# Strassen moved between products of two interleaved layers: input product of the last FFN in all four chunks, K instead of Q in layer 2

## The chip, the cores and the metric

The kernel runs on one core of a Trainium2 chip. The metric is the device time of one execution in microseconds (us), as the median of several executions; lower is better. Profiles are of one execution each. Some executions of a program come out slower, with a lower granted clock in the records. Every ratio is of fast executions alone.

In the text PE is TensorE, PEld its weight loads, DVE is VectorE, ACT is ScalarE, POOL is GpSimd and SP is SyncE, which issues the DMA transfers.

## The reference, cut to what matters

```python
def reference(A_x, A_wqkv, A_wo, B_x, B_w1, B_w2):      # x: 1 x 2048 x 512, bf16; w1: 512 x 1376
    def _A_ref(x, wqkv, wo):                             # linear attention, 32 heads of 16
        q, k, v = ...                                    # x @ wqkv
        phi = lambda t: jnp.where(t > 0, t + 1, jnp.exp(t)) + 1e-6
        pq, pk = phi(q), phi(k)
        kv = jnp.einsum("bhsd,bhse->bhde", pk, v)
        z = jnp.einsum("bhsd->bhd", pk)
        num = jnp.einsum("bhqd,bhde->bhqe", pq, kv)
        den = jnp.einsum("bhqd,bhd->bhq", pq, z)[..., None] + 1e-6
        return ...(num / den) @ wo
    def _B_ref(x, w1, w2):
        return jnp.maximum(x @ w1, 0) @ w2
    x = A_x
    x = x + _A_ref(_layernorm(x), A_wqkv, A_wo)          # layer 0
    x = x + _B_ref(_layernorm(x), B_w1, B_w2)            # layer 1
    x = x + _A_ref(_layernorm(x), A_wqkv, A_wo)          # layer 2
    x = x + _B_ref(_layernorm(x), B_w1, B_w2)            # layer 3, "the last FFN"
    return x
```

## The kernel before

The 2048 rows are four chunks of 512. The kernel first records all operations with what they read and write. A table in the source (`ORDER`) then gives the order in which they are dealt out to the engines, another (`BANKS`) the PSUM bank of each accumulator, and the waits follow from the data and the banks. Each engine runs its own list strictly in that order.

Some products are done by one level of Strassen: 7 block products of half the size in place of 8. The block sums of x and of the weights and some of the outputs cost DVE and ACT work. This is one group of the FFN's Strassen product (layer 3 did chunks 1 to 3 so, chunk 0 plain):

```python
f32s = [(lden[:, 0, :], ...), (lden[:, 1, :], ...), (rhi ... F32, ...), (rsp[:]....bitcast(F32), [("rsp", 0), ("rsp", 1)])]

def f32_slot(layer):                     # scratch for the copy c6, taken in turn
    L = f32s[1:] if layer == 1 else f32s
    ...
tt(0, blk(0, 0), blk(0, 1), ALU.add, TK[0])              # tb0: block sums of the transposed x, on DVE
tt(1, TS[0], blk(1, 1), ALU.subtract, TK[1] + tk[0])     # tb1
...
X, Z = alloc_bank(full), alloc_bank(full)
prod("p1", w_raw(0, 1), t_sum(0), X, True)               # PE
prod("p6", w_sum(4), t_raw(1, 1), Z, True)               # PE
s6, k6 = f32_slot(layer)
copy(lambda: s6[:, 0:W], Z, [], k6, "c6")                # PSUM -> scratch, ACT or DVE
Y = alloc_bank(full, seeded=True)
copy(bank_ap(Y), X, [], [("ps", Y)], "c11")              # PSUM -> PSUM
prod("p2", ..., X);  prod("p5", ..., Y);  relu(Y, 0, 0)
V = alloc_bank(full, seeded=True)
g.add(DVE, ... psv[:, V] = psv[:, X] + s6 ...)           # c21
prod("p4", ..., X);  prod("p3", ..., V);  relu(V, 1, 0)
U = alloc_bank(full, seeded=True)
copy(bank_ap(U), X, ..., "c12")
g.add(DVE, ... out_ap(1, 1) = pv(X) + s6 ...)            # hadd: frees bank X
g.add(DVE, ... max(out_ap(1, 1), 0) ...)                 # hq
prod("p7", ..., U);  relu(U, 0, 1)
```

An operation's name carries its chunk and the first feature tile of its group: hadd0_0 is the hadd of chunk 0, first group. Q and K of attention have the same scheme.

Of the kernel before, what the change touches and what calls it, by code (L numbers as in the profile page):

```python
# [9 lines left out]
F32 = mybir.dt.float32  # L10
# [122 lines left out]
17 0 14 12 15 18 13 1 16 19 2 20 22 3 24 4 21 23 25 5 6 26 27 7 28 8 29 40 30 33 31 32a 41 34 47 42 35 71 43 36 48 44  # L133
49 37 45 50 73 38 46d 72 51 81 74 39a 75 52 54 82 76 53a 60 83 86 58 78 56 87 77 79 61 57 55 98 59 89 62 84 63 119 88
93 99 115 100 108 64 66d 95 65d 67a 103 80 69 117 68a 92 85 90 94 113 70 135 105 91 104 116 120 141 114 118 121 110
180 122 109 251 174 130 176 123 136 132 127d 124d 131 125d 142 138 126d 128 178 137 148 143 179 133 181 129 175 144
169 177 134 182 149 96 183 106 159 111 171 112 170 97 147 107 160 101 161 184 191 185d 186a 187d 139 164 140 150 189
172 192 153 173 165 151 239 188d 193 154 102 190 166 145 162 203 155 163 167 156 9 152 209 194 10 205 157 195 11 204
197 146 210 158 196 206 199 207 198 240 221 200 168 211 201 215 223 212 213 222 233 224 217 225 216 227 218 234 219
235 202 428 228 208 229 236 237 252 230 231 253 427 254 214 255 322 282 323 242 220 283 243 226 324 241 284 232 325  # L140
245 285 238 244 246 326 250 247 259a 329 248 249 257d 256a 260 286 258a 287 270 262 327 289 261 280 263 328 330 272
264 288 271 265 281 290 314 267 273 320 291 275 315a 333 331 321a 318 268 316 277 319d 294 317a 332 266 309 293 274
296 292 395 311 269 278 310 297 400 396 295 276 397 410 401 398a 279 405 402 411 403a 339 412 406 413a 415 334 407 340
408a 383 335 343 349 416 341 336 338 337d 344 350 342a 299 351 353 345 354 384 429d 304 346 352d 301 347d 433 300 424
355 434 436a 465 430d 306 466 449 425 435a 450 305 426 437 468a 438 385 356 298 421 312 451a 431d 386 470 348 432d 469
369 471d 439a 302 422d 399 371 307 423 303 404 377 372d 467a 414 389 440 363 388 378a 308 442 390 364a 313 441 472 387
443a 357 481 370d 444a 473 474 417 409 358 375 359 445 475a 476a 447 446 418 482 393 373 477 376a 392 365 483 394 448d
374a 484 367 452a 391 478 366a 419 498 368d 420 493 499 486 502 503 494 487 500 497 508 485 501d 495 488 504 496a 381
509 507 513 379 510 512 490 505 506d 479 511a 454 491 453 489 382a 514 515 360 380a 492 456 480a 519 361a 545d 455a
524 362 520 529 525 523 546d 566 528 534 567a 530 549 533 547d 458 550a 548d 603 459a 457 604a 598d 568 460a 599d 551  # L150
569 602 552 570 461 553 571 605a 463 554 572 462 464a 601d 555 535 573a 618 556a 674d 538 607 578 526 608a 675d 561
527a 600d 606 521 621d 522a 562 609 579 539 563 677d 557 574 564 580 558 581 565 678 559 575 679a 622 582 576 680 560
623 681 634 536 624a 583 682 637d 577 537d 610 683 638 613a 611 584 531 585 532d 639 612a 684 586 676d 540 587 640a
616 685a 614 695 617a 619 588 751d 696a 595 591d 620a 615 592a 697 625 690 596a 698 594 589a 627 516 590d 626 628a
752d 635 593 699 754d 636a 753d 629a 686 700 691 630 597 701 641 632 702a 631 642 517 541 633a 643 518 542 687 644d
692 707 645a 693 703 646 694 648 647 708 649a 688 755 803d 689 662 758a 804d 756 664 772 757a 805d 704 759 773a 709
806d 663 760 807 761a 705 650 808a 762 706 771 710 652 763 651 774d 809 711 712 764 766d 775 765a 810 769 665 713 811
770a 714 715 666 716 776 812 656 777a 778 717 813 719a 720d 780 814d 658 779 543 767 544 718a 819 653 781d 824 782a
722 787 654 657 815 783 825a 785 659 668 790d 786a 721d 792 768 670 723 791 793d 826 669 784 660 816 748 827 817 828
749a 671 818 788 829 724 750 789d 794 830 726 672 796 725 831d 795 820 797d 798a 727 832 728 836 799 837 800 801 730  # L160
802a 873d 736 732 731 874d 821 833 738 838 655 737 875d 877 876d 661 822 667 834 878a 823 839 879 835 894 880 840 673
895d 841 842 843 881 733 844 734 845 896 882 729 897 739 846 898 849d 850a 848d 883 847d 852 735 899 884d 900 740 851
1066 889 1065 890 1068 1067 885 901d 891 902 892 886 903 893 887 742 904 888 906 744 907 743 908 745 868 905 909 746
910 741 911 912 1069 869 747 913 914 870 915 858 871 872 943 916 860 920d 853 859 919d 861 922 958 855 862 918d 854
863 917d 959 856 921 960 944 857 865 948 961 864 962 953 866 950 867 949 933 951 954 952 955 968 935 956 934 928 957
936 937 969 930 929 923 931 932 938 924 925 945 939 970 926 940 927 963 941 942 980 965 964 946 966 982 971 967 981
947 983 972 984 985 973 995 974 987 975 1000 986 988 997 1001 989 996 1070 998 990 999 1071 978 1002 992 976 991 979
1005 993 1004 1072 1025a 977 1006 994 1003 1024a 1027 1023d 1026a 1073 1011 1029 1009 1047 1028 1030 1007 1012 1074
1048 1075 1077a 1010 1049 1013 1076d 1051 1078 1050a 1008 1053 1014 1055 1031 1054a 1032 1052d 1056d 1037 1034 1084
1033 1133 1039 1035 1015 1036 1038 1123 1017 1134 1018 1135 1118 1124 1016 1136a 1040 1128 1127 1125 1119 1126a 1019  # L170
1085 1120 1129 1042 1121a 1130 1022 1091a 1086 1138 1021 1044 1079 1020 1131d 1097 1043 1045 1182 1087 1139 1041 1046
1081 1167 1183 1080 1088 1184 1057 1168 1098 1172 1099 1169 1170d 1177 1058 1173 1137 1174 1147 1175d 1059 1100 1187
1082 1122 1149 1089 1090 1148a 1178 1159 1132 1060 1150d 1185a 1155 1179 1101 1180a 1083 1161 1092 1156a 1188 1196d
1151 1093 1162d 1094 1216 1189 1140 1152a 1063 1141 1200 1095 1171 1062 1096 1157 1142 1061 1203d 1160a 1143 1064
1219d 1106 1158a 1153 1107 1197d 1176 1163 1199d 1104 1154a 1165 1103 1108 1164d 1181 1201 1109 1102 1166a 1144 1105
1198d 1202a 1204 1300d 1186 1205 1207 1220 1145a 1232 1206a 1111 1193 1302d 1113 1235a 1217 1301d 1194a 1110 1208
1218a 1112 1209 1303d 1195 1236 1210a 1221 1223 1319 1222a 1146 1190 1248 1191 1117 1211a 1192 1115 1225 1114 1212
1224 1226a 1214 1116 1320a 1253 1213 1215a 1249 1321 1227a 1250 1251d 1237 1252 1258 1322 1254 1238a 1230 1255 1257
1323 1256d 1259 1231a 1263 1268 1324 1262 1304 1260 1264 1325 1265 1267 1261d 1233 1279 1305d 1326a 1266d 1234a 1228
1306 1269 1327 1307 1239 1330 1338d 1308 1280 1331 1309 1283 1241 1229 1240 1242d 1310 1243a 1281 1282a 1339d 1274  # L180
1311d 1244 1342 1275 1246 1343 1247a 1340d 1315 1345a 1245 1341d 1344a 1284 1390d 1278 1312 1285 1316 1391d 1288 1347
1276 1346 1392d 1277a 1358 1328 1349 1348a 1317 1294 1313 1332 1393d 1361a 1350 1351 1286 1333 1363 1352a 1362 1270
1364a 1271 1287d 1394 1353a 1272 1318 1273 1359 1329 1356 1360a 1289 1428d 1395a 1365 1357a 1396 1290 1366 1354 1335
1369a 1293 1397 1367 1291 1374 1336a 1292d 1398 1355 1368a 1295 1296 1372 1399 1375 1370 1377a 1400 1373a 1337 1379
1376d 1401a 1409 1371 1380a 1297 1405 1298 1314 1410a 1299 1402 1432 1411 1334 1429d 1435a 1431d 1378 1433 1412 1406
1430d 1434a 1413 1381 1437 1414 1382 1438a 1383 1415 1384a 1385d 1436 1416a 1386 1465 1403 1466a 1407 1387 1449 1404
1448 1450a 1439 1388 1420 1389a 1408 1451a 1421 1480d 1441 1440 1442a 1482d 1452 1443a 1464 1481d 1453 1467a 1417
1454a 1444 1446 1484 1447a 1445 1455 1422 1469 1485a 1468 1483d 1470a 1457 1418 1458a 1423 1499 1486 1471 1500a 1419
1456 1473 1487 1501 1424 1459a 1472 1474a 1502 1488 1460 1425 1461 1475a 1503 1489 1426a 1476 1462 1427 1490 1477
1463a 1504 1478 1517d 1491a 1505 1479a 1495 1506a 1515d 1496 1510 1516d 1497 1511 1498 1519 1518d 1534 1520a 1507  # L190
1535a 1521 1536 1522 1508 1537 1512 1523 1509 1538 1524 1492 1539 1513 1525 1540 1526a 1493 1541a 1530 1494 1527 1514
1528 1542 1529 1543 1545 1554 1544 1546 1531 1547 1555 1532 1548 1549 1533 1550 1551 1553 1552
# [1265 lines left out]
```

## Time and profile before

| | before |
|---|---|
| time, median (range) | 271.12 us (270.93 to 271.31, 3 runs) |
| span of the profiled execution | 269.3 us |
| granted PE clock | 1.0 |
| DVE / ACT busy | 86% / 73% |

PE is busy 98% of the span. Because shown matmul times overlap, this document counts PE otherwise: from the start of one group's first weight load to the start of the next group's, less the turns of its matmuls (216 ns for 512 columns, 109 for 256; the prediction derives both from the timeline). What is left over is **waiting**. PE's own work in before is 259.3 us by this count and its waits come to 5.5 us, of which 3.1 us lie before 11 us, while inputs arrive. Weight loads serve for it because none of their records is missing. The count has an artefact: about 0.3 us at each group of small denominator products (their turn is uncertain), in all kernels alike, except where such a group lies at the border of two stages: it can then be counted on either side, and this is said. Only differences between kernels are used.

A line of a timeline gives start us, length us, engine, line, operation, output and inputs, count; in brackets the idle time before it and its releaser.

```profile
199.09 0.42 DVE L964 TENSOR_TENSOR xn<-xn,Tb 128x512 f16<-128x512 f16 x1 [1.06 <-DMA Tb<-xn]
...
197.79 2.76 PE L539 MATMUL ps<-Tb,w 128*128 128x512 bf16 x12
```

DVE stood 1.06 us, from 198.0 to 199.1, for a transposing transfer. PE did not notice: it was in the middle of twelve plain products of FFN chunk 0, which need nothing but transposed x and weights.

### The profile page before, as it was taken

How to read it: one execution, taken by the hardware profiler on the slowest of the kernel's cores; microseconds unless marked ns; L12 is line 12 of the kernel's file. 1: busy time of each engine (PE TensorE's matmuls, PEld its weight loads, DVE VectorE, ACT ScalarE, POOL GpSimd, SP SyncE). 2: the span in 40 equal slices, each digit the busy share in tenths (PEclk: the TensorE clock that was granted, in tenths of full speed). 3: DMA queues.
4: the chain of work that ended last, by engine and by line, in shares of the span. 5: the costliest groups of instructions: out<-in, count | busy, mean ns of one | idle time of the engine just before them, and what ended most of it. 6: DMA issues, size and time to landing. Idle time of an engine off the chain costs nothing.

```text
span 269.3 us, 5317 instructions
## 1 busy us (share of the span) xinstructions
PE 263.8 (98%) x1973; PEld 170.5 (63%) x1973; DVE 232.6 (86%) x635; ACT 196.1 (73%) x426; POOL 18.8 (7%) x30
## 2 busy tenths in 40 slices
PE   7999999999999999999999999999999999999995
PEld 2444454447556879778666544455458677888884
DVE  4999975999989999999799765599989999979865
ACT  3889956999978768787542887899998757656420
POOL 4111000000110002111010100000011001100000
PEclk9999999999999999999999999999999999999999
DMA  6954973254343027204004060215356222320204
GB/s 209 382 112 79 241 259 102 93 80 99 97 134 63 2 40 87 52 1 80 19 2 78 0 82 1 74 57 126 78 139 118 41 39 41 58 82 0 100 0 156
DMA packets 47481, 23.60 MB, mean 88 GB/s; under 512 B 36736, under 2 KB 46048, under 8 KB 47456
## 3 DMA queue, kind: packets, MB, share of 16 engines
q1 hardware_dynamic: 47312, 23.21, 35.1%
q8 instruction: 15, 0.25, 0.4%
q14 instruction: 10, 0.08, 0.1%
q10 hardware_dynamic: 144, 0.07, 0.1%
HBM read 11.21 MB, written 3.15 MB: 53 GB/s over the span
## 4 chain that ended last, share of the span: by engine, by line
PE 92%; DVE 3%; DMA 3%; ACT 1%; issue 0%
PE ps L539 92%; DMA Tb<-xn 2%; DVE bst L446 1%; DMA xin<-in_A_x_dram 1%; DVE xn L478 0%; DVE xn L579 0%; ACT sqscr L546 0%; DVE xn L1166 0%; PE ps L502 0%; DVE mv L447 0%; ACT escr L521 0%; ACT big L519 0%; DVE Tb L510 0%; DVE big L525 0%; DVE xn L1126 0%
## 5 line engine op out<-in xcount | busy, mean ns | idle before, releaser
L521 ACT ACTIVATE escr<-ps 128x512 bf16<-128x512 f32 x60 | 35.7, 606 | 7.8 <-PE ps L539 7.8
L546 ACT ACTIVATE sqscr<-xres 128x512 bf16<-128x512 f32 x48 | 30.4, 634 | 14.5 <-DVE xres L583 7.6
L519 ACT ACTIVATE big<-ps 128x512 bf16<-128x512 f32 x60 | 35.1, 606 | 1.0 <-PE ps L539 1.0
L539 PE MATMUL ps<-wqkv,Tb 128*128 128x512 bf16 x128 | 31.2, 379 | 1.0 <-DMA Tb<-xn 0.5
L1015 ACT ACTIVATE big<-ps 128x512 bf16<-128x512 f32 (+1 forms) x47 | 24.9, 536 | 9.6 <-PE ps L539 8.8
L539 PE MATMUL ps<-big,xn 128*128 128x512 bf16 x128 | 30.9, 379 | 0.0
L539 PE MATMUL ps<-gw,big 128*128 128x512 bf16 x128 | 30.3, 379 | 0.0
L539 PE MATMUL ps<-Tb,wqkv 128*128 128x512 bf16 x112 | 27.0, 379 | 0.0
L525 DVE TENSOR_TENSOR big<-big,escr 128x512 bf16<-128x512 bf16 x60 | 24.6, 421 | 2.4 <-ACT big L519 1.5
L523 DVE TENSOR_SCALAR escr<-escr 128x512 bf16<-128x512 bf16 x60 | 16.9, 287 | 9.2 <-ACT escr L521 8.8
L539 PE MATMUL ps<-w2s,big 128*128 128x256 f16 x160 | 21.9, 273 | 0.0
L539 PEld LDWEIGHTS ps<-wqkv,Tb 128*128 128x128 bf16 x128 | 12.0, 98 | 14.6 <-DMA Tb<-xn 1.0
L539 PEld LDWEIGHTS ps<-big,xn 128*128 128x128 bf16 x128 | 12.2, 98 | 13.8 <-issue 0.4
L539 PE MATMUL ps<-w,big 128*128 128x256 f16 (+2 forms) x113 | 20.6, 302 | 0.0
L539 PEld LDWEIGHTS ps<-gw,big 128*128 128x128 bf16 x128 | 12.2, 98 | 12.8 <-issue 0.5
L539 PE MATMUL ps<-w,xin 128*128 128x256 bf16 (+1 forms) x140 | 19.5, 273 | 0.0
L539 PE MATMUL ps<-xn,xin 128*128 128x256 f16 x128 | 19.5, 272 | 0.0
L998 ACT ACTIVATE ps<-ps 128x512 f32<-128x512 f32 (+1 forms) x28 | 14.6, 521 | 5.7 <-PE ps L539 2.8
L539 PEld LDWEIGHTS ps<-Tb,wqkv 128*128 128x128 bf16 x112 | 10.8, 98 | 12.5 <-issue 0.2
L539 PE MATMUL ps<-xn,w 128*128 128x256 f16 x120 | 18.7, 273 | 0.0
L539 PE MATMUL ps<-Tb,w 128*128 128x512 bf16 x80 | 18.4, 379 | 0.0
L539 PE MATMUL ps<-Tb,wper 128*128 128x256 bf16 x120 | 18.3, 273 | 0.0
(152 smaller groups left out, 512.0 us busy)
## 6 DMA issues: line engine op xcount, KB each, us to landing
xn<-rdram SPq DMA_DIRECT2D x32, 128.0 KB
wqkv<-in_A_wqkv_dram SPq DMA_DIRECT2D x3, 512.0 KB, 7.2
xin<-in_A_x_dram SPq DMA_DIRECT2D x3, 512.0 KB, 8.0
out_dram<-xn SPq DMA_DIRECT2D x3, 512.0 KB, 2.6
w<-in_B_w_dram SPq DMA_DIRECT2D x1, 1376.0 KB, 6.7
w<-in_B_w_dram SPq DMA_DIRECT2D x1, 1280.0 KB, 9.8
rdram<-rsp SPq DMA_DIRECT2D x8, 128.0 KB, 1.7
wo<-in_A_wo_dram SPq DMA_DIRECT2D x1, 512.0 KB, 10.2
```

What stands on the lines that cost most here:

```text
L446: g.add(DVE, lambda e: e.bn_stats(bst[:, i, :], xin[:, i, :]), [("xin", i)] + list(behind), [("bst", i)], C_DVE_BNST, name="bnst%d" % i)
L519: g.add(ACT, lambda e: e.activation(dst_ap, psv[:, b, :], ACTF.Identity, bias=1.0 + 1e-6, scale=1.0), [("ps", b)], [dst_key], C_ACT_PSUM, ...
L521: g.add(ACT, lambda e: e.activation(escr[:, s, :], psv[:, b, :], ACTF.Exp), [("ps", b)], [("escr", s)], C_ACT_EXP, name=name + "_exp")
L523: g.add(DVE, lambda e: e.tensor_scalar(escr[:, s, :], escr[:, s, :], 1.0, 1e-6, ALU.min, ALU.add), [("escr", s)], [("escr", s)], C_DVE_BF4 ...
L525: g.add(DVE, lambda e: e.tensor_tensor(dst_ap, dst_ap, escr[:, s, :], ALU.max), [dst_key, ("escr", s)], [dst_key], 340.0, name=name + "_phi")
L539: last = e.matmul(o, l, r, start=st, stop=sp, skip_group_check=skip)
L546: g.add(ACT, lambda e: e.activation(sqscr[:, q, :], xres[:, i, :], ACTF.Square, accum_out=dst[:, i:i + 1]), [("xres", i)], [("sqscr", q), ...
L998: g.add_flex([(ACT, lambda e: e.activation(dst(), psv[:, src, 0:W], ACTF.Identity), cost(C_ACT_PSUM)), (DVE, lambda e: e.tensor_copy(dst() ...
L1015: g.add_flex([(ACT, lambda e: e.activation(out_ap(r, m), pv(b), ACTF.Relu), cost(C_ACT_PSUM)), (DVE, lambda e: e.tensor_scalar(out_ap(r, m ...
```

## The change

The intent is fewer PE turns: Strassen also for chunk 0 of the last FFN's input product, K of layer 2 by Strassen in chunks 2 and 3, Q of chunk 3 of layer 2 plain again. The order, the banks and some scratch places go with it. The core of the diff, with cuts marked:

```diff
 ORDER = """                       # all 1600 operations in a new order; BANKS likewise
...
-QSTR=(3,), ... KSTR=(), ... HSTR=[(1, 2, 3), (1, 2, 3)]
+QSTR=(), ... KSTR=[(), (2, 3)], ... HSTR=[(1, 2, 3), (0, 1, 2, 3)]
...
-   ... 750.0 * (hi - lo), "tr%d" % lo, issue=C_SP_TR)      # guess of a transpose's transfer, for the order only
+   ... 950.0 * (hi - lo), "tr%d" % lo, issue=C_SP_TR)
...                                                         # sums and scratch of K get places of their own:
+   home = [xn[:, 4 * t + k, :] if kind == "q" else unit_ap(pq_unit(k, t)) for k in range(4)]
...
+   else:
+       s6 = big[:].bitcast(F32).rearrange("p (c t k) -> p c t k", t=NCH, k=256)[:, 8:10, 2, :]
...
-                        if layer == 2 and t in KSTR:
+                        if t in KSTR[layer // 2]:
```

## The prediction

> **What bounds the kernel now.** I began with the busy shares of the page.
>
> ```profile
> PE 263.8 (98%) x1973; PEld 170.5 (63%) x1973; DVE 232.6 (86%) x635; ACT 196.1 (73%) x426; POOL 18.8 (7%) x30
> ...
> PEclk9999999999999999999999999999999999999999
> ```
>
> The TensorE (PE) is busy nearly always, at full clock in every slice. A busy PE can still be starved, because the shown time of a matmul is longer than its turn in the pipeline. So next I read the chain that ended last, in order of time:
>
> ```profile
> 9.88 139.47 PE ps L539 x1014
> ...
> 153.79 4.55 DMA Tb<-xn
> 158.34 0.04 issue
> 158.38 107.37 PE ps L539 x849
> 265.75 0.02 issue
> 265.78 0.75 DVE xn L579
> 266.53 0.39 DVE xn L1126
> ```
>
> From 9.9 us on the end is set by matmuls alone, except for one break at 149 to 158 us, where layer 1 ends and the last LayerNorm tiles are normalised and transposed. What that break costs stands in the PE timeline; whether PE is starved between matmuls can be read from pure runs of one shape there:
>
> ```profile
> 156.03 1.89 PE L539 MATMUL ps<-Tb,wqkv 128*128 128x512 bf16 x8
> 158.38 1.04 PE L539 MATMUL ps<-wqkv,Tb 128*128 128x512 bf16 x4 [0.47 <-DMA Tb<-xn]
> ...
> 190.44 5.34 PE L539 MATMUL ps<-Tb,w 128*128 128x512 bf16 x24
> ...
> 257.60 1.25 PE L539 MATMUL ps<-w,xin 128*128 128x256 bf16 x10
> ```
>
> The columns are start, length, engine, line, operation, tiles, shapes, count. The only visible idle time after the start is 0.47 us before the K projection of the last chunk. A run's length is (count - 1) turns plus one shown duration. The groups give 379 ns shown for a 512-wide and 273 ns for a 256-wide matmul, so a turn is (5.34 - 0.379)/23 = **0.216 us** for 512 columns and (1.25 - 0.273)/9 = **0.109 us** for 256. Those are the turns in runs that wait for nothing. Start to start in the whole trace, the medians are the same 216 and 109 ns, and all turns longer than that by over 40 ns add up to 4.3 us of excess, some 1.6 us of it before 10 us and 0.64 us at the break. PE is therefore bound by its own work: each turn taken away is worth its full length, unless a wait appears.
>
> What the other engines have to spare depends on the stage. Windows of the two last layers, with DVE (VectorE) and ACT (ScalarE) busy time in the fourth and fifth group:
>
> ```profile
> core 0: us, PE busy (x) PEld busy (x) DVE busy (x) ACT busy (x) POOL busy (x), PEclk, DMA share, GB/s
> 140.00:165.00 25.00, 24.53 (x182) 13.82 (x180) 19.12 (x58) 15.91 (x33) 2.18 (x2) 1.00 0.29 43
> 165.00:180.00 15.00, 15.00 (x107) 7.61 (x105) 10.56 (x28) 11.96 (x23) 0.00 (x0) 1.00 0.16 54
> 180.00:200.00 20.00, 20.00 (x111) 9.88 (x109) 18.25 (x60) 19.30 (x42) 1.01 (x1) 1.00 0.45 112
> 200.00:215.00 15.00, 15.00 (x137) 11.41 (x136) 14.76 (x40) 12.77 (x31) 1.11 (x1) 1.00 0.42 82
> ```
>
> K of layer 2's last chunks runs at 147 to 164 us, Q of chunk 3 at 176 to 189, and the plain first chunk of the last FFN at 190 to 200. There both DVE and ACT are over 90% busy.
>
> **What the Trainium skill says.** "TensorE: Matmul & The Clock Gate", section "Wait — 56ns, not 53.3ns?", gives start to start as N / 2.4 GHz plus about 2.5 ns: 215.8 ns for 512 and 109.2 for 256. The trace agrees (216 and 109). It also says why Strassen gains a little less than an eighth here: twice as many narrower matmuls pay the fixed part twice as often. "Perfetto Trace Analysis", section "Identifying the Most-Contended Engine", warns that matmul busy time does not tell the headroom of TensorE; so I rest on the turns, not on the 98%. "VectorE: DVE Perf Modes", section "The perf-mode tier table (the rule you actually need)", puts a 16-bit two-tensor operation in SBUF at two elements per cycle and one with an operand in PSUM at one. The trace agrees: 0.42 us for the 128x512 sums of 16-bit blocks, 0.69 us for the adds that read PSUM (turns of 0.34 and 0.61 back to back). So the block sums are the cheap part of a Strassen product, and the PSUM copies and adds are the dear part.
>
> **The change, part by part.** One Strassen level replaces 8 block products by 7, and each 512-wide matmul by 256-wide ones.
>
> Input product of the last FFN, chunk 0 (the others have it already): 10 feature tiles x 4 = 40 wide matmuls go, 7 x 10 = 70 narrow ones come: 40 x 0.216 - 70 x 0.109 = 8.64 - 7.63 = **1.01 us less**. Its weight sums have been kept since layer 1, so none are added. DVE and ACT gain four block sums (4 x 0.34 = 1.4). Each of two full groups gains three PSUM copies (1.5), an add from PSUM for the seed and one for the output (1.2) and a small ReLU (0.2), and loses one of four ReLUs (0.5): 2.4 each. The half group comes to 1.6. In all about 7.8 us.
>
> K in chunks 2 and 3 of layer 2: per chunk 16 wide for 28 narrow: 3.46 - 3.05 = 0.40, so **0.81 us less**. DVE and ACT gain five weight sums (1.7) and, per chunk, four block sums (1.4), three copies (1.5) and two adds (1.2): 1.7 + 2 x 4.1 = 9.9 us.
>
> Q of chunk 3 in layer 2 goes back to plain: **0.40 us more** on PE, and 1.7 + 4.1 = 5.8 us less on DVE and ACT.
>
> PE sum: -1.01 - 0.81 + 0.40 = **-1.41 us** (56 wide matmuls fewer, 98 narrow ones more). DVE and ACT together: 7.8 + 9.9 - 5.8 = 12 us more, on 428.7 us now, or 82% of the two engines' time instead of 80%: no new bound on the whole.
>
> The order of all instructions and their banks is replaced too. The arithmetic of the other stages isn't touched, so the same turns should come in another order; the order was made with a longer guess for a transpose's transfer (950 for 750 ns a tile). That should hide some of the 0.64 us at the break: I take 0.3 off.
>
> **Rivals.** *The vector engines become the bound locally.* At 180 to 200 us they have 37.6 of 40 us in use. The Q part leaves there (-4.1; its weight sums were at 144 to 151 us), the FFN part comes (+7.8): 41.3 of 40. Against it: at 165 to 180 only 22.5 of 30 are used, and at 200 to 215 27.5 of 30, so a reordering can spread it. If it can't, 1.3 us over two engines is 0.65 us of stall, and twice that where one engine alone is in the way: the total then stands at 270.5 to 271.
>
> *The K products become a chain.* Plain K needs only its own pair of transposed tiles; a Strassen chunk needs all four tiles, then block sums, seeds copied in PSUM, then the rest, with four of the eight banks held by the accumulators of phi(K) and x. After the last transpose lands at 158.4 that may cost 2 to 3 us more of latency. Against it: PE has other work that doesn't need this K, namely the accumulation of eight held-back tiles (8 x 4 x 0.216 = 6.9 us) and the Q chunks (3.5 us each). DVE and ACT have room there: 35 of 50 us at 140 to 165, and 43 with the change. I expect at most 0.5 us of stall; if the fillers are spent early, 2 us and a total near 272.
>
> *A gain that is hidden anyway*, if the break at 149 to 158 were a fixed delay that saved PE work before it can't shorten. Only K of chunk 2 could lie before it, 0.40 us, and the stall itself is 0.6, so little can vanish so.
>
> **Range and chances.** 271.12 - 1.41 - 0.3 for the break + 0.5 for new stalls of the first two rivals, an estimate = **269.9 us**. Without new stalls it would be 269.4, with a lucky order at the start (up to 1.6 us of excess is there) 269. With both rivals at their middle it would be 271.3. I take 268.9 to 271.3 for 8 in 10. The 2% line is 5.4 us away on either side; PE's removable stalls are under 4.3 us in all, so faster by over 2% would need nearly all of them gone as well: 0.01. Slower by over 2% needs 7 us of new stalls in an order that somebody chose: 0.02. Within 2%: 0.97.
>
> **What would show it.** In the changed profile the plain FFN group (Tb with w, 512 wide) should stand at 40 instead of 80, K (wqkv with Tb) at 96 instead of 128, Q at 128 instead of 112, with turns of 216 and 109 ns as before; PE's busy time should fall by 1 to 1.5 us and its share stay 98%. DVE plus ACT should rise by about 12 us. If the first rival is right, gaps on PE released by ACT or DVE show between 185 and 215 us; if the second, PE waits at 158 to 168 us for DVE block sums or PSUM seeds. The prediction is wrong if the reordering moved waits into stages that the change doesn't touch, which the shapes can't tell, or if the turns of the narrow matmuls there are longer than 109 ns because their weight loads or banks come late.

## More of the kernel before

The denominator of attention goes through DRAM to be spread over partitions.

```python
def a_den_inv(t, b):                      # chunk t
    mm_group(... "den%d")                                             # PE: four small products
    g.add(ACT, lden[:, s] = ln(psum + eps));  g.add(ACT, rsp[:, s] = exp(-lden[:, s]))
    dma(r <- rsp[:, s], "rw%d")                                       # 128 KB to DRAM
    for j in range(4):
        dma(xn[:, 4 * t + j] <- r[32 * j:32 * j + 8] broadcast, "rb") # and back, 128 KB each
def a_den_mul(t, s, GB):
    for j in range(4):
        g.add(DVE, u_j = u_j * xn[:, 4 * t + j], name="us%d_%d")      # what the wo product reads
```

So the scratch of Strassen's c6 and the buffer that the denominators are written to DRAM from are the same memory (rsp).

## The result, and the profile after

| | before | after |
|---|---|---|
| median (range), same rounds | 271.17 us (270.93 to 271.31, 4 runs) | 271.09 us (270.50 to 271.32, 4 runs) |
| ratio after / before | | 0.9995, 95% interval 0.9976 to 1.0013 |
| span of the profile, granted clock | 269.3 us, 1.0 | 269.5 us, 1.0 |

The result is correct. A ratio is the mean time of one kernel's fast runs over the mean of the other's fast runs of the same rounds, so it isn't quite the ratio of the medians. No gain was measured where 1.2 us had been forecast.

First the busy shares of the page and three groups of PE (output and inputs, shapes, count, then busy us and mean ns):

```profile
PE 262.7 (98%) x1994; PEld 174.2 (65%) x2015; DVE 237.6 (88%) x650; ACT 201.9 (75%) x441; POOL 18.8 (7%) x30
...
L541 PE MATMUL ps<-Tb,wqkv 128*128 128x512 bf16 x128 | 30.4, 379 | 0.0
...
L541 PE MATMUL ps<-wqkv,Tb 128*128 128x512 bf16 x91 | 22.8, 379 | 0.7 <-DVE Tb L512 0.2 <-ACT Tb L511 0.2
...
L541 PE MATMUL ps<-Tb,w 128*128 128x512 bf16 x40 | 9.1, 379 | 0.0
```

The plain FFN group is at 40 and Q at 128, as forecast. K shows 91 of 96, because 21 matmul records are missing from this trace (2015 weight loads, 1994 matmuls). DVE and ACT together rose by 10.8 us against 12 forecast. PE's own work, counted by turns over the program's list of matmuls, is 257.9 us: **1.40 us less**, as forecast. So the whole gain is there, and 1.6 us of waits came to it.

The chain that ended last shows where (start us, us, what):

```profile
56.06 4.82 DMA Tb<-xn
60.91 0.43 DVE xn L977
...
152.95 8.69 PE ps L541 x95
...
179.49 6.87 PE ps L541 x31
186.38 0.60 ACT escr L523
...
193.26 3.97 DMA xn<-rdram
...
198.03 0.59 DVE big L1049
...
204.17 0.62 DVE ps L1042
204.84 7.78 PE ps L541 x58
...
220.21 45.74 PE ps L541 x414
```

The break at 149 to 158 us is gone; matmuls run through it. In its place the chain leaves PE from 186 to 205 us, for ACT, DVE and a broadcast (xn from rdram) that took 3.97 us, and once at 56 us, for a transpose of 4.82 us. Before, both stretches were matmuls.

Waits of PE by stage, from the count described above (us):

| | own work | 0–11 | 11–56 | 56–72 | 72–142 | 142–183 | 183–218 | 218–end | all waits |
|---|---|---|---|---|---|---|---|---|---|
| before | 259.3 | 3.06 | 0.41 | 0.07 | 0.35 | 1.08 | 0.33 | 0.20 | 5.5 |
| after | 257.9 | 3.22 | 0.36 | 0.56 | 0.31 | 0.57 | **1.78** | 0.32 | 7.1 |

This is the whole account of the profiled executions: -1.40 own work, +1.45 at 183–218, +0.49 at 56–72, -0.51 at 142–183, +0.2 elsewhere. The sum is +0.2, and so is the difference of the spans.

The PE timeline at 183–218 shows single gaps, not a slower pace:

```profile
186.96 2.76 PE L541 MATMUL ps<-gw,big 128*128 128x512 bf16 x12 [0.29 <-DVE big L862]
...
196.19 0.61 PE L541 MATMUL ps<-Tb,wper 128*128 128x256 bf16 x4
197.04 0.85 PE L541 MATMUL ps<-w,Tb 128*128 128x96 bf16 x16 [0.24 <-ACT rsp L1011]
...
200.35 0.60 PE L541 MATMUL ps<-Tb,xin 128*128 128x256 bf16 x4
201.09 0.61 PE L541 MATMUL ps<-Tb,wper 128*128 128x256 bf16 x4
```

From matmul to matmul the waits are 0.35 us before the wo product at 187, 0.41 at 197.0 and 0.30 at 201.1. (At 200.35 four turns of 109 ns take 0.44 us, yet the next group starts 0.74 us later.) The engines that released them were waiting themselves:

```profile
196.60 0.38 ACT L1011 ACTIVATE rsp<-ps 128x256 f32<-128x256 f32 x1 [0.47 <-DMA rdram<-rsp]
...
197.26 0.42 DVE L862 TENSOR_TENSOR big<-big,xn 128x512 bf16<-128x512 bf16 x1 [0.89 <-DMA xn<-rdram]
...
199.28 0.43 DVE L862 TENSOR_TENSOR big<-big,xn 128x512 bf16<-128x512 bf16 x1 [0.33 <-DMA xn<-rdram]
```

ACT wanted to copy a Strassen block into rsp (c6), and the denominators' write out of rsp had not ended. DVE stood for broadcasts with the two multiplies of chunk 2; behind them in its list was hadd0_0, whose PSUM bank PE needed at 201 us. Those writes out of rsp, over the whole run (minimum, median, maximum from issue to landing), first before, then after:

```profile
DMA to landing us min/median/max: 1.7/1.7/2.2
```

```profile
DMA to landing us min/median/max: 1.7/1.7/3.9
```

The windows with DVE and ACT busy in the fourth and fifth group show how full both were:

```profile
180.00:200.00 20.00, 19.32 (x142) 12.00 (x142) 18.51 (x62) 19.19 (x44) 0.00 (x0) 1.00 0.50 117
200.00:215.00 15.00, 14.75 (x126) 11.29 (x127) 13.96 (x39) 13.77 (x36) 1.51 (x1) 1.00 0.26 49
```

DVE worked 18.51 of 20 us and stood 1.22 for the two broadcasts; ACT worked 19.19 and stood 0.47 for the write. Neither had more than 0.4 us of other slack. But they had been as full before: 18.25 and 19.30 us in this window (the lines stand in the prediction). Together that is 37.6 us before and 37.7 after, not the 41.3 that the first rival had counted. Of the 10.8 us that came on the whole, 6.5 came at 140 to 165 us. So the waits came without more work in this window.

### The profile page after: what moved, and what is told of

The parts are those of the page before. It is cut to its first block, busy times and chain, and to the rows that moved or that the text cites. A ratio compares the mean times of both kernels' runs of the same rounds, so it can differ in the third digit from the quotient of the medians.

```text
span 269.5 us, 5414 instructions
## 1 busy us (share of the span) xinstructions
PE 262.7 (98%) x1994; PEld 174.2 (65%) x2015; DVE 237.6 (88%) x650; ACT 201.9 (75%) x441; POOL 18.8 (7%) x30
## 4 chain that ended last, share of the span: by engine, by line
PE 86%; DVE 6%; DMA 3%; ACT 3%; issue 1%; SPq 0%
PE ps L541 84%; DMA Tb<-xn 2%; PE ps L425 2%; DMA xn<-rdram 1%; ACT sqscr L548 1%; DVE xn L977 1%; DVE xres L554 1%; DVE ps L1042 1%; ACT ps L1011 1%; DVE xin L948 1%; DVE big L1049 0%; DVE big L862 0%; ACT lden L846 0%; PE ps L504 0%; ACT rsp L848 0%
## 5 line engine op out<-in xcount | busy, mean ns | idle before, releaser
L523 ACT ACTIVATE escr<-ps 128x512 bf16<-128x512 f32 x56 | 33.1, 611 | 6.4 <-PE ps L541 5.9
L1028 ACT ACTIVATE big<-ps 128x512 bf16<-128x512 f32 (+1 forms) x53 | 27.0, 533 | 8.7 <-PE ps L541 8.0
L541 PE MATMUL ps<-Tb,wqkv 128*128 128x512 bf16 x128 | 30.4, 379 | 0.0
L541 PE MATMUL ps<-wqkv,Tb 128*128 128x512 bf16 x91 | 22.8, 379 | 0.7 <-DVE Tb L512 0.2
L541 PE MATMUL ps<-xn,xin 128*128 128x256 f16 x140 | 21.7, 273 | 0.0
L541 PE MATMUL ps<-Tb,wper 128*128 128x256 bf16 x140 | 21.0, 273 | 0.1
L541 PE MATMUL ps<-xn,w 128*128 128x256 f16 x140 | 20.9, 273 | 0.2 <-DVE xn L977 0.2
L1111 ACT ACTIVATE ps<-ps 128x256 f32<-128x256 f32 x26 | 9.5, 369 | 13.6 <-PE ps L541 11.8
L1011 ACT ACTIVATE ps<-ps 128x512 f32<-128x512 f32 (+1 forms) x35 | 18.2, 532 | 0.8 <-PE ps L541 0.3
L541 PEld LDWEIGHTS ps<-w2s,big 128*128 128x128 bf16 x160 | 15.4, 98 | 4.3 <-DVE xres L1106 0.4
```

The source lines that it names most:

```text
L523: g.add(ACT, lambda e: e.activation(escr[:, s, :], psv[:, b, :], ACTF.Exp), [("ps", b)], [("escr", s)], C_ACT_EXP, name=name + "_exp")
L541: last = e.matmul(o, l, r, start=st, stop=sp, skip_group_check=skip)
L1011: g.add_flex([(ACT, lambda e: e.activation(dst(), psv[:, src, 0:W], ACTF.Identity), cost(C_ACT_PSUM)), (DVE, lambda e: e.tensor_copy(dst() ...
L1028: g.add_flex([(ACT, lambda e: e.activation(out_ap(r, m), pv(b), ACTF.Relu), cost(C_ACT_PSUM)), (DVE, lambda e: e.tensor_scalar(out_ap(r, m ...
L1111: g.add_flex([(ACT, lambda e: e.activation(psv[:, c1, cols], psv[:, c2, L], ACTF.Identity), 290.0), (DVE, lambda e: e.tensor_copy(psv[:, c ...
```

## The experiments

The theory after the result: the Strassen product of FFN chunk 0 puts DVE and ACT work, in a fixed sequence, between PE's own products where both engines are full, and their waits for transfers reach PE. The rivals: the shared scratch; the particular order (then another order would have the gain); something that has nothing to do with chunk 0, as at 56–72 us. Sixteen kernels ran. The waits of the profiled execution of each (us, as above):

| | own work | 0–11 | 56–72 | 142–183 | 183–218 | all waits |
|---|---|---|---|---|---|---|
| before | 259.3 | 3.06 | 0.07 | 1.08 | 0.33 | 5.5 |
| after | 257.9 | 3.22 | 0.56 | 0.57 | 1.78 | 7.1 |
| a_scratch | 257.9 | 2.93 | 0.39 | 0.57 | 1.61 | 6.6 |
| a_light | 257.9 | 2.87 | 0.47 | 0.57 | 1.19 | 6.4 |
| a_both | 257.9 | 3.29 | 0.26 | 0.57 | 0.93 | 6.2 |
| a_dve0 | 257.9 | 3.41 | 0.26 | 0.57 | 1.81 | 7.0 |
| a_dve | 257.9 | 3.69 | 0.33 | 0.57 | 1.51 | 7.1 |
| a_dve2 | 257.9 | 2.81 | 0.54 | 0.57 | 1.53 | 6.6 |
| a_late | 257.9 | 2.97 | 0.57 | 0.47 | 1.96 | 7.0 |
| a_early | 257.9 | 2.90 | 1.66 | 0.57 | 1.39 | 6.9 |
| b_tail | 259.3 | 3.24 | 0.38 | 0.21 | 0.45 | 5.9 |
| a_tail | 257.9 | 3.05 | 0.28 | 0.54 | 1.28 | 6.4 |
| h_tail | 258.3 | 3.16 | 0.38 | 0.28 | 1.62 | 6.4 |
| k_tail | 258.9 | 3.06 | 0.08 | 0.21 | 0.96 | 6.2 |

How much such a number varies can be seen in a_early: its order from 75 us on is that of after, and it still shows 1.39 for 1.78 us. So 0.4 us in one stage of one execution proves nothing; the start alone moves by 0.9.

Two things that the table hides matter for the four tail kernels. First, the artefact: in a_tail a group of small products lies right at 183 us, so about 0.3 us of it is counted in 142–183, where before and after have it in 183–218; in b_tail and h_tail about 0.3 us fall into 56–72, where before has it in 11–56. Counted weight load by weight load, without the artefact, the waits at 183–218 lie above those of before by 1.45 us in after, 0.11 in b_tail, 1.25 in a_tail, 1.29 in h_tail, 0.49 in k_tail and 0.60 in a_both. Second, the stage 72–142 is left out. It has 0.35 us of waits in before and 0.31 in after, but 1.23 in b_tail, 0.59 in a_tail, 0.55 in h_tail and 1.44 in k_tail: losses of the new orders that have nothing to do with the change.

**a_scratch: the scratch apart.** The c6 blocks of the last FFN go into weight memory that nobody reads any more.

```diff
-            L = f32s[1:] if layer == 1 else f32s
+            L = f32s[1:] if layer == 1 else [(wqkv[:, n, 0:1024].bitcast(F32), [("s6w", n)]) for n in range(4)]
```

(The copy also names the last Q products, so that it waits for the weights' last readers.)

> The changed kernel with one edit: the f32 scratch of the last FFN's Strassen products lies in the columns of the Q and K weights, free by then, instead of in the buffers that the denominators of layer 2 use too. Same instructions, order and banks. Theory (new waits at 183 to 203 us ate the gain): the ScalarE wait of 0.47 us for the write of the denominators, and the 0.41 us that PE loses behind it, vanish; at most 0.4 us less, 270.7, and about 0 if the next wait (VectorE behind the broadcasts) takes its place. Rival (the narrow products themselves cost more than counted): no change, 271.1.

Correct, 270.69 us, ratio to before 0.9983 (0.9969 to 0.9998). The wait of 0.41 us at 197 is gone, but PE then waited 0.64 us for hadd0_0 where it had waited 0.30 in after. DVE and PE of this kernel:

```profile
195.65 0.42 DVE L977 TENSOR_TENSOR xn<-Tb 128x512 f16<-128x512 bf16 x1 [0.75 <-DMA Tb<-xn]
...
198.76 0.42 DVE L862 TENSOR_TENSOR big<-big,xn 128x512 bf16<-128x512 bf16 x1 [0.49 <-DMA xn<-rdram]
...
200.56 0.61 PE L541 MATMUL ps<-Tb,wper 128*128 128x256 bf16 x4 [0.49 <-DVE big L1049]
```

The next transfer in DVE's list took the place of the one removed. The sharing is real, but alone it is worth little.

**a_light: less work.** In FFN chunk 0 alone, the PSUM copies, adds and ReLUs handle 32 of each 256 columns. Order, buffers and dependencies are unchanged.

```diff
+                light = layer == 3 and t == 0
+                def cut(ap):   # as it is unless light; else [:, :, 0:32] of the (j, 256) view
-   ... e.activation(dst(), psv[:, src, 0:W], ACTF.Identity)
+   ... e.activation(cut(dst()), cut(psv[:, src, 0:W]), ACTF.Identity)     # and the other five likewise
```

> Wrong result on purpose. The changed kernel, but the PSUM copies, adds and ReLUs of the last FFN's chunk 0 work on 32 of each 256 columns; count, order, banks and all matmuls as they are. Theory (VectorE and ScalarE, over 90% busy there, cannot take the 8 us of new work, so PE waits): PE's excess at 183 to 218 us falls from 1.8 us to under 1, the time by 0.6 to 1.2 us to about 270.2. Rival (DMA broadcasts and the shared scratch set the waits, not the amount of work): under 0.3 us less. Rival (narrow products): no change.

Wrong result (relative error 0.27), 270.61 us, ratio 0.998 (0.9961 to 0.9998). The window and one line of ACT:

```profile
180.00:200.00 20.00, 19.55 (x146) 12.36 (x144) 16.63 (x62) 15.93 (x45) 0.00 (x0) 1.00 0.52 117
```

```profile
196.36 0.20 ACT L1020 ACTIVATE rsp<-ps 128x32 f32<-128x32 f32 x1 [0.98 <-DMA rdram<-rsp]
```

DVE and ACT did 5.1 us less there, and the waits at 183–218 fell to 1.19. But ACT, now early, waited longer for the shared buffer (0.98 for 0.47 us), and PE still waited 0.34 us behind it (0.41 in after). The result lies between what the theory (waits under 1 us, 0.6 to 1.2 us less) and its first rival (under 0.3 us less) had expected. Load alone doesn't explain all either.

**a_late and a_early: the order of one stretch sought anew.** Only `ORDER` and `BANKS` differ: in a_late for the operations at about 175 to 220 us, in a_early for those at about 48 to 75 us. A few copies also moved between ACT and DVE.

```diff
-ORDER = """ ... 1541 ... """        # after's
+ORDER = """ ... """                 # a_late: positions 1041 to 1345 permuted; a_early: 290 to 450
```

> The changed kernel with the same instructions and arithmetic, only those between about 175 and 220 us in another order, where the rest of layer 2 is not done before the first FFN products but among them. Theory: the loss sits in this stage, so 1 to 1.8 us less, 269.3 to 270.1, and PE's excess at 183 to 218 us falls from 1.8 us to under 0.6. Rival (narrow products, or waits spread all over): within 0.3 us of 271.1.

> The changed kernel with the same instructions, only those between about 48 and 75 us, in layers 0 and 1 that the change does not touch, in another order. Theory: 0.5 us of the loss comes from the new order here (PE's excess at 56 to 72 us is 0.56 us against 0.07 before), so 0.4 to 1.0 us less, 270.1 to 270.7, with the waits at 183 to 218 us left as they are. Rival (all of it lies at the end of layer 2): no change, 271.1.

Both correct; a_late 271.26 us, ratio 1.0008 (0.9993 to 1.0023); a_early 271.38 us, 1.0017 (0.9996 to 1.0038). Neither helped. The search went by durations taken from the trace and did not foresee transfers that land late when others run; in a_early the first block sum of layer 1 waited for a transpose, and PE for 1.04 us of that. These are misses of the method: they don't show that no better order exists.

**b_order, a_order, h_order, k_order: a whole new order (failed).** To compare parts of the change without the accident of one order, four kernels got an order from one method: b is before's arithmetic, a is after's, h adds only FFN chunk 0 to before, k only K for Q.

```diff
 b_order: QSTR=(3,), KSTR=(),            HSTR=[(1, 2, 3), (1, 2, 3)]
 a_order: QSTR=(),   KSTR=[(), (2, 3)],  HSTR=[(1, 2, 3), (0, 1, 2, 3)]
 h_order: QSTR=(3,), KSTR=[(), ()],      HSTR=[(1, 2, 3), (0, 1, 2, 3)]
 k_order: QSTR=(),   KSTR=[(), (2, 3)],  HSTR=[(1, 2, 3), (1, 2, 3)]
```

> The arithmetic of the kernel before, with the order and the banks of all instructions sought anew, by one method for this and the next three: the turns and wait times of this case's traces, each transfer taken at the slowest that was seen. PE's own work stays 259.3 us. Theory (the order, not the number of products, decides how much of the work shows as time): PE's excess of 5.5 us falls to 3 to 4.5, the time to 268.5 to 270. Rival (the order before was already as good as the chip allows): 271.1.

> The arithmetic of the changed kernel, order and banks sought anew by the same method. PE's own work 257.9 us. Theory (the 1.41 us are there, only covered by the waits of the shipped order): 1.0 to 1.5 us less than b_order. Rival (the added PSUM copies and adds cost PE as much in waits as seven products for eight save, in any order): within 0.4 us of b_order.

> One part alone: the last FFN's input product by Strassen in all four chunks, K and Q as before; order sought anew by the same method. PE's own work 258.3 us. Theory: 0.7 to 1.0 us less than b_order. Rival (the stage at the end of layer 2 cannot take this part): no less than b_order.

> The other part alone: K of layer 2 by Strassen in chunks 2 and 3 and Q without it, the last FFN as before; order sought anew by the same method. PE's own work 258.9 us. Theory: 0.2 to 0.5 us less than b_order, which is about as much as five rounds can tell. Rival (K by Strassen delays the end of layer 1 or the start of Q): 0.3 us more than b_order.

All correct and all slower: 277.64 (ratio 1.0236), 275.48 (1.0156), 283.13 (1.0412) and 279.52 us (1.0312). The new orders spoiled the start, where inputs arrive: waits before 56 us were 7 to 14 us, against 3.5 in before. The profile of h_order also fell in the slow state (clock 0.98). They say nothing on the parts of the change.

**b_tail, a_tail, h_tail, k_tail: before's order up to 72 us, the rest by one method.** The parameters are those of the four above; the first part of `ORDER` is before's own.

> The first four reorderings lost 3 to 12 us in the first 72 us, where the loads of the inputs land, so this set keeps the order of the kernel before up to 72 us and seeks only the rest anew, by one method for all four. This one has the arithmetic of the kernel before: PE's own work 259.3 us. Theory (before, PE waited for hardly anything after 72 us, so there is nothing to win): within 0.5 us of the kernel before, 270.7 to 271.6; excess at 183 to 218 us about 0.4 us.

> The arithmetic of the changed kernel with the order of before up to 72 us, the rest sought anew. PE's own work 257.9 us. Theory: the 0.5 us lost at 56 to 72 us are back, and half or more of the waits at 183 to 218 us: 0.7 to 1.4 us less than b_tail, 269.7 to 270.4. Rival (the last FFN's chunk 0 by Strassen makes PE wait there in any order): excess at 183 to 218 us again over 1.4 us, and no more than 0.5 us less than b_tail.

> One part alone: the last FFN's product by Strassen in all four chunks; K and Q as before (Q of chunk 3 by Strassen, just ahead of it); order of before up to 72 us, the rest sought anew. PE's own work 258.3 us. Theory (VectorE and ScalarE are the limit at 183 to 218 us, and the Q products that lie there are not removed): excess at 183 to 218 us the largest of the four, over 1.5 us, and no gain against b_tail. Rival (the waits come from the order, not the load): excess under 0.8 us and 0.6 to 1.0 us less than b_tail.

> The other part alone: K of layer 2 by Strassen in chunks 2 and 3, Q without it, the last FFN as before; order of before up to 72 us, the rest sought anew. PE's own work 258.9 us. Theory: excess at 183 to 218 us at most that of b_tail, 0.2 to 0.6 us less than b_tail, the whole of its 0.40 us. Rival (the K products are a chain that PE waits for at 142 to 183 us): excess there 0.4 us or more above b_tail, and no gain.

All correct, on one chip, before at 271.36 us:

| | median | ratio to before (95%) | own work | waits at 183–218 |
|---|---|---|---|---|
| b_tail | 271.64 | 1.0011 (0.9985 to 1.0037) | 259.3 | 0.45 |
| a_tail | 271.04 | 0.9984 (0.9961 to 1.0006) | 257.9 | 1.28 |
| h_tail | 271.21 | 0.9988 (0.9963 to 1.0014) | 258.3 | 1.62 |
| k_tail | 271.84 | 1.0013 (0.9991 to 1.0035) | 258.9 | 0.96 |

With before's arithmetic the method's order has 0.45 us of waits at 183–218, as before's own has 0.33. With FFN chunk 0 by Strassen it has 1.28 and 1.62; without the artefact both come to about 1.6 on the scale of before's 0.33. So the waits are not an accident of the one order that came with the change. The 0.96 of k_tail, which has chunk 0 plain, is 0.8 on that scale, and 0.51 us of it stand before the wo product at 187 us, which waited there for the denominator multiplies on DVE.

The windows of b_tail and a_tail, DVE and ACT again in the fourth and fifth group:

```profile
180.00:200.00 20.00, 19.95 (x123) 10.17 (x122) 19.47 (x61) 18.38 (x41) 0.00 (x0) 1.00 0.47 102
```

```profile
180.00:200.00 20.00, 19.41 (x136) 11.51 (x135) 19.41 (x63) 17.97 (x39) 0.00 (x0) 1.00 0.45 123
```

Both are about equally full (37.9 and 37.4 of 40 us), and the waits of PE differ by 1.1 us. In a_tail DVE stood for no transfer at 183 to 210 us, and the write out of rsp landed within 2.1 us at most. So neither more work in the window nor a late transfer is needed for these waits. What differs is that PE's products of chunk 0 need what those engines make.

From b_tail to a_tail the means fall by 0.27%, or 0.7 us. The intervals overlap, so this is a tendency and not shown by the times alone; and in the profiles 0.64 us of it are the difference of the two orders at 72–142. At 183–218 a_tail loses 1.1 us more than b_tail, so little of its 1.4 us of saved work is left. The times expected for a_tail (269.7 to 270.4) were missed; its rival's waits of over 1.4 us came, without the artefact. For h_tail the waits came as expected. K for Q alone (k_tail) shows no gain, although PE's work falls by 0.4 us: its waits rose at 183–218, against its theory, and not at 142–183, against its rival.

**a_both: a_light and a_scratch together.** The edits are those two; the order is after's.

> Wrong on purpose: a_light (a quarter of the work of the copies, sums and ReLUs of FFN chunk 0) and a_scratch together, order unchanged. In a_light 0.44 us of wait for the shared scratch and 0.35 us behind the queue stayed. If those are what kept a_light from more, waits at 183 to 218 us go from 1.19 to 0.6 to 0.8 and the time to 270.0 to 270.3; if load alone matters, nothing changes against a_light (270.6).

Wrong (0.27), **270.31 us with before at 271.31, ratio 0.9957 (0.9934 to 0.998)**: by the ratio 1.2 us below before, as much as the prediction had forecast for the change. The ratio is 0.0038 below that of after, and the two half-intervals together make 0.003 (root of the sum of squares, an estimate), so the difference is beyond this noise. Waits at 183–218 are 0.93, the lowest of all kernels with chunk 0 by Strassen, though 0.6 to 0.8 had been expected. PE at the places where after had waited:

```profile
195.87 0.60 PE L541 MATMUL ps<-Tb,wper 128*128 128x256 bf16 x4
196.31 0.84 PE L541 MATMUL ps<-w,Tb 128*128 128x96 bf16 x16
...
199.61 0.60 PE L541 MATMUL ps<-Tb,xin 128*128 128x256 bf16 x4
200.13 0.60 PE L541 MATMUL ps<-Tb,wper 128*128 128x256 bf16 x4
```

Four turns of 109 ns are 0.44 us, and so is the first step; the last step is 0.52. With room on DVE and ACT and the buffer apart, these gaps close. The wait before the wo product stays (0.28 us shown idle, 0.29 in after), so it belongs neither to the copies of chunk 0 nor to the shared buffer. And the room is large: DVE and ACT worked 32.7 us at 180 to 200, against 37.6 in before. The run shows where the gain was lost; it doesn't show that a correct kernel could have it.

**a_dve0 and a_dve: VectorE's order by hand.** Five operations move so that DVE doesn't stand for transfers with hadd0_0 behind them; nothing else changes. a_dve0 is on after, a_dve on a_scratch.

```diff
-... cen3 us1_3 ... tb0_1 c21_0_0 us2_1 c21_0_4 hadd0_2 us2_2 us2_0 hrelu0_1_0_0 hadd0_0 ...
+... us1_3 cen3 ... c21_0_0 c21_0_4 tb0_1 hadd0_2 hrelu0_1_0_0 hadd0_0 us2_1 us2_2 us2_0 ...
```

> The changed kernel with the same instructions; only VectorE's order of five of them is moved between 184 and 201 us: one centring (cen3) behind the last denominator multiply of chunk 1, the first block sum of FFN chunk 1 (which stood 0.75 us for a transpose in a_scratch) and three denominator multiplies of chunk 2 (which stood 0.89 and 0.33 us for their broadcasts in the changed kernel) behind the Strassen sum hadd0_0 whose bank TensorE waits for. Theory (VectorE's queue stands in order behind transfers that land late, and TensorE waits for what is queued behind them): the waits of 0.35 us at 186 and 0.41 us at 200 us go, the 0.6 us at 196 us (shared scratch) stay; waits of TensorE at 183 to 218 us from 1.78 to about 1.0, time 270.2 to 270.6. Rival (VectorE and ScalarE simply have too much work there): what is moved comes back as a wait a little later, waits stay at 1.6 or more, time 271.0.

> The same moves of VectorE's order on top of a_scratch (scratch of the last FFN's Strassen blocks apart from the denominators' buffer). If the two causes are separate and both are real: waits at 183 to 218 us from 1.78 (changed kernel) and 1.61 (a_scratch) to 0.5 to 0.9, time 269.8 to 270.2, below a_scratch by 0.5 to 0.8. If load is the cause: within 0.2 of a_scratch, about 270.7.

Both correct; a_dve0 270.99 us, ratio 0.9987 (0.9957 to 1.0016); a_dve 270.81 us, 0.9975 (0.9953 to 0.9997). In a_dve DVE no longer waits for any transfer between 184 and 206 us, and the gap at the wo product is gone. But gaps stayed or came elsewhere: PE waited 0.32 us at 189.8 (0.10 in after) for a Q map of chunk 3 that now stood behind cen3, still 0.21 at 200.7 for hadd0_0, and 0.18 at 201.8 for tb1_1, which stood behind the three multiplies. Waits at 183–218 were 1.81 and 1.51, for 1.78 and 1.61. The order theory expected 0.5 to 0.9 for a_dve; its rival, that the wait comes back elsewhere, held.

**a_dve2: more moves.** On a_dve, the operations that its remaining gaps named were moved ahead, or what stood before them behind. Six more operations (not seven, as the text below says) change place, one of them at 64 us, besides the three multiplies that make way.

```diff
-... resid5 q3_3_phi q3_2_phi ... hadd0_0 us2_1 us2_2 us2_0 tb1_1 tb3_1 tb2_1 ... c21_1_0 hadd0_4 us2_3 ...
+... q3_3_phi q3_2_phi resid5 ... hadd0_0 tb1_1 tb3_1 tb2_1 us2_1 us2_2 us2_0 us2_3 ... c21_1_0 hadd0_4 ...
-... tb1_1 c11_1_0 wa1_1 ...        # layer 1, 64 us
+... tb1_1 wa1_1 c11_1_0 ...
```

> a_dve with seven more of VectorE's operations moved by hand so that those TensorE waits for come first: the residual of chunk 1 behind the Q maps of chunk 3 (wait of 0.52 us at 188 us in a_dve), three block sums of FFN chunk 1 ahead of the denominator multiplies of chunk 2 (0.28 us at 201 us), the last multiply of chunk 2 earlier (0.18 us at 204 us), and a weight sum of layer 1's FFN ahead of a copy (0.25 us at 64 us). If waits that remain in a_dve are a matter of order, they fall by 0.6 to 0.9 us in all and the time to 269.9 to 270.3. If the work is what holds, they come back elsewhere and the time stays at 270.6 to 270.9.

Correct, 271.43 us with before at 271.98 on that chip (both scattered more there), ratio 0.9991 (0.9968 to 1.0015). The gaps aimed at closed, and others opened behind the operations that had made way:

```profile
64.03 0.61 PE L540 MATMUL ps<-xn,xin 128*128 128x256 f16 x4 [0.36 <-DVE ps L1011]
...
203.60 0.61 PE L540 MATMUL ps<-xn,w 128*128 128x256 f16 x4 [0.50 <-DVE ps L1041]
```

From matmul to matmul these are 0.53 us (c11_1_0, now behind a weight sum) and 0.66 us (c21_1_0, now behind four multiplies). No correct version was found that has the forecast gain: a_dve (0.9975, or 0.7 us below before) and a_scratch (0.9983) are the best, and their intervals overlap that of after.

## Why the prediction was right or wrong

- **Bound by PE, turns of 216 and 109 ns, -1.41 us of own work:** right. Counted, it is 1.40, with the same turns after.
- **12 us more for DVE and ACT:** nearly; 10.8 were measured.
- **The break at 149 to 158 us, "I take 0.3 off":** right in kind; waits at 142–183 us fell by 0.51. The transposes landed at 152.6 and 153.9 us (before: 158.3 and 159.1). The third rival thus fell. An order can win this without the change: b_tail, with before's arithmetic, has only 0.21 us of waits there.
- **The second rival, K as a chain:** did not come. The chain shows matmuls only from 153 to 179 us.
- **The step that failed** is the term "+ 0.5 for new stalls of the first two rivals, an estimate". It was mis-sized: the new stalls at 183–218 us came to 1.45 us. The first rival had named the place, both engines and even the size ("0.65 us of stall, and twice that where one engine alone is in the way"), but the prediction gave it less than its smaller figure because "a reordering can spread it". (Its total, "270.5 to 271", is a slip: 269.4 plus 0.65 to 1.3 is 270.1 to 270.7.) The reordering did spread the work, 37.7 us in the window for 37.6 before, and the stalls came all the same. So it was wrong to count a stall as work beyond the 40 us of the window. In the tail series the waits follow FFN chunk 0 in orders made anew, by 1.1 us at equal load of the two engines; in a_both, where chunk 0's copies, adds and ReLUs are cut to an eighth of their columns and the sharing is gone, the forecast gain appears; hand moves of the order (a_dve, a_dve2) only passed the waits on. What the window count left out is that DVE and ACT lists are in order and nearly full, in after with 1.22 us of standing for transfers on top of 18.51 of work. Before, plain products of chunk 0 covered this: DVE stood 1.06 us at 199 us and PE ran on. Strassen made the very products dependent on DVE and ACT. No run varied this dependence alone; the nearest is b_tail against a_tail, in one profile each.
- **Not all of the 1.45 us is of chunk 0.** The 0.35 us before the wo product stands in a_both too, and k_tail, with chunk 0 plain, waits 0.51 us there.
- **Waits moved "into stages that the change doesn't touch":** named as what would make the prediction wrong, and given no number. It was 0.49 us at 56–72 us in the profiled execution, where DVE stood 0.45 us for the transpose of 4.82 us. Waits there were 0.26 to 0.57 us in all kernels with after's order of that stretch; b_tail, h_tail and k_tail, with before's order there, have 0.07 to 0.08 when the artefact is left out, a_tail 0.28.

The four terms, -1.40 - 0.51 + 1.45 + 0.49, make 0.03 us, with 0.2 more in the start and the rest, which varies between executions by more than that. The prediction came to -1.2; the 271.09 us measured lie 1.2 us above its 269.9, near the upper end of its range.

What stays open: how the waits at 183–218 divide between load and sharing. a_light (0.998) and a_scratch (0.9983) differ too little from after (0.9995), and the same order can differ by 0.4 us there in one execution. Only both together stand out. How much late transfers add stays open too: after has eight broadcasts and a DMA share of 62% at 186 to 202 us, before four and 49%, and no run changed that alone. Whether some order keeps the gain with the full work also stays open; six attempts by search or hand did not find one.

## What to carry to other kernels

In these traces a product that needs nothing but loaded operands was a filler for its engine: it covered the waits of the others. Before replacing it by one with fewer turns and more side work, count the time in which the side engines stand for transfers as well as their busy time, and count as gain only what that stage can feed. Here 1.0 us of PE turns in FFN chunk 0 was bought with 7.8 us of DVE and ACT work by the forecast's count, in a window (180 to 200 us) where those two had 2.4 of 40 us left.

When a gap names its releaser, moving that operation ahead helps only if what makes way isn't waited for too. Sum the waits of the whole stage after each move.

## What the Trainium skill lacked or had wrong

- "DMA: Bandwidth & Descriptors", section "Anatomy of one DMA — SWDGE (gpsimd) path", fits one DMA as about 2.0 us plus bytes over 436 GB/s, which for 128 KB would be an estimate of 2.3 us, for transfers issued by GpSimd. Here 128 KB writes to DRAM issued from SP took 1.7 us as a median, and up to 3.9 us in after, among broadcasts and transposes of the same core. Its section "Latency and other measured facts" says that HBM latency grows with load, which fits the direction; no page gives a size for a core's own transfers delaying each other.
- The same page, section "DMA Transpose (X-bar)", has no time from issue to landing for small transposes. Here those of two 128x512 tiles took 3.0 to 4.9 us from issue to landing, with a median of 3.2.
- "Perfetto Trace Analysis", section "Optimization Strategy", says to find the gaps of the bound engine and make what they wait for start sooner or complete faster. With VectorE and ScalarE both over 90% busy, starting it sooner did not help: ten such moves changed the waits of the stage from 1.61 to 1.53 us, because what made way was waited for too. The page doesn't warn of that.
- No page on traces says that matmul records can be missing: here a trace holds 1994 of 2015. Counting by weight loads and by the program's list settles it.
